# Scales of weights and tokens from sums of squares on ScalarE, and token operands turned in smaller DMAs, in a fused attention and mixture-of-experts kernel

## The chip, the cores and the metric

The kernel runs on one core of one Trainium2 chip. The metric is the time of one execution on the device in microseconds (us), as the median of several runs. PE is the matrix engine (TensorE), PEld its loads of weights, DVE is VectorE, ACT is ScalarE, POOL is GpSimd, and SP is the engine whose queue issues most DMAs. L1244 is line 1244 of the kernel before. The clock that PE was granted is given as a share of full speed, 2.4 GHz; its lower level is 1.2 GHz.

## What is computed

A windowed attention over 8 batches, 8 heads, 576 positions and 64 channels gives `x` of 4608 tokens by 512. Each token then goes to the two best of 8 experts, by noisy logits; an expert is a two-layer network of 512 to 1024 to 512, and a token's two results are added with its two weights. Cut to what matters here:

```python
scores = np.where(mask, scale * q @ k.T + bias, -1e9)      # window of 128 positions
attn = np.exp(scores - scores.max(-1)); attn /= attn.sum(-1) + 1e-9
x = (attn @ v)                                              # 4608 x 512
top2 = np.argpartition(-noisy_logits, 2, axis=1)[:, :2]
for e in range(8):
    for k in range(2):
        mask = top2[:, k] == e
        h = np.maximum(x[mask] @ w1[e], 0.0)
        out[mask] += top2_w[mask, k, None] * (h @ w2[e])
```

## The kernel before, in words

The products of the experts run in float16. An operand is scaled by a power of two and split into a high and a low half, so that hi*hi + hi*lo + lo*hi comes near to a product in float32. A scale must be known before anything can be split. For an expert's two weight matrices it is one number per matrix: `size_of_weights` (L1223) loads them once more in eight pieces of 128x1024 (`mraw`, a ring of two tiles), `largest` (L1230) takes the largest absolute value of each row of a piece on DVE (L1244), `powers_of_weights` (L1249) takes the maximum over all partitions with the help of PE (`of_all`, L484) and `floor_powers` (L495) keeps the exponent. For tokens it is one number per row: `turn_pair` (L1305) takes it for two gathered tiles of 128 tokens at a time, by a maximum on DVE (L1333).

Every expert but the first has three blocks of tokens: two wide ones of 512 and a narrow rest. A wide block's first product is done with seven smaller products in place of eight, by sums and differences of quarters of its operands. So `turn_pair` forms three more quarters (L1327 to L1331) on DVE or POOL, whichever the plan chooses, scales and splits 4 + 3 quarters into `hi` and `lo` tiles of 128x1792 (tiles `th`, `thw`, `tlw`; a ring of two pairs), and `across` (L1398) has SP issue one transposing DMA for each of the two tiles, 14 chunks of 128 columns at once, into the operand `blk.x` (tiles `xhw`, `xlw` or `xhe`, `xle`). Two pairs make a wide block, so that a block's operands come by four such DMAs.

In the products, `up_wide` (L1443, matmuls at L1434) writes banks that DVE and ACT add up and empty (`first_sum` to `halves_of`, lines 1479 to 1528: tiles `c`, `hh` and `hl`; line 277 is ACT's copy and line 279 DVE's), and `downs` (matmuls at L1564) multiplies `hh` and `hl` by the second weights. The narrow block's matmuls are at L1408 and L1569. Weights of an expert are loaded in chunks (`raw`, L1270 on SP's queue), scaled and split (L279 or L277 for the high half, L1276 for the low half, L1126 and L1141 for sums of them) into twelve sets of tiles, of which an expert takes eight.

The order on each engine isn't left to a scheduler. At build time the class `Order` plays the program through with estimated durations: a step is a strand of a coroutine that asks for an engine with a rank, the ready request with the lowest rank is issued first, and what comes out is the fixed order of every engine and of SP's queue. Ranks are numbers at the head of the file (`STAGE`, `GATE`, `SIZES`, `LATE`, ...), and durations stand beside each request. `either` (L261) and `added` let the plan choose between ACT and DVE, or DVE and POOL. On the chip every engine runs its rows strictly in that order and waits where a semaphore isn't there yet.

## Time and profile before

| | us |
|---|---|
| median of 3 runs | 1077.29 (1075.73 to 1081.77) |
| the profiled execution, its own time | 1077.1 |
| span of that execution, first to last instruction | 1075.4 |
| PE busy | 975.8 (91%) |
| DVE busy | 897.6 (83%) |
| ACT busy | 495.8 (46%) |
| POOL busy | 552.2 (51%) |
| mean granted clock of PE | 0.977 of full speed |

The profiled execution lies within 0.2 us of the median. Attention and routing take about the first 210 us, the first expert (in three blocks of its own, narrower kind) goes to about 330 us, and the seven others, about 100 us each, go on to the end. Busy shares are means over parts with different limits, so the stretches in which PE stands idle are read one by one below.

### The profile page before, as it was taken

What the parts mean: (1) busy time and instruction counts of PE and PEld (TensorE: products, weight loads), DVE (VectorE), ACT (ScalarE), POOL (GpSimd) and SP (SyncE); (2) the same over time, 40 slices, a digit from 0 to 9 for tenths busy, and PEclk for the clock granted to TensorE, in tenths of its full rate; (3) what the DMA queues carried; (4) which work ended last, traced back from release to release, by engine and by line L of the source; (5) the groups of instructions that cost most, each with busy time, mean ns of one, the idle gap of its engine ahead of it and who ended that gap; (6) DMA issues with size and microseconds to landing.
All of it is one profiled execution on the core that took longest, in us unless ns stands there. A gap on an engine that the chain in (4) does not pass through costs nothing. (4 is left out here: it accounts for less than half of the span.)

```text
span 1075.4 us, 24441 instructions
## 1 busy us (share of the span) xinstructions
PE 975.8 (91%) x8656; PEld 670.7 (62%) x8656; DVE 897.6 (83%) x2655; ACT 495.8 (46%) x1364; POOL 552.2 (51%) x767
## 2 busy tenths in 40 slices
PE   8999999799787899989988999899789989989996
PEld 5776666565356666766666656666656676657663
DVE  8999999997558999889799979998688979898530
ACT  8997987742123534353334333433433353434221
POOL 3458786654242456465464445555456456464022
PEclk9999999999898999999989999999999999998998
DMA  8869889642898499685969497857986897967023
GB/s 321 277 213 302 296 251 346 172 134 41 223 181 164 111 220 201 112 222 156 167 131 215 136 180 174 202 156 141 114 234 165 157 196 205 140 137 130 11 40 48
DMA packets 234540, 188.82 MB, mean 176 GB/s; under 512 B 145264, under 2 KB 188560, under 8 KB 234416
## 3 DMA queue, kind: packets, MB, share of 16 engines
q1 hardware_dynamic: 217072, 148.30, 53.7%
q0 software_dynamic: 17344, 38.94, 19.6%
q8 instruction: 68, 1.11, 0.4%
q14 instruction: 56, 0.46, 0.1%
HBM read 116.24 MB, written 40.71 MB: 146 GB/s over the span
## 5 line engine op out<-in xcount | busy, mean ns | idle before, releaser
L1668 POOL DMA_INDIRECT out_dram<-yo,ix x69 | 120.2, 1742 | 125.9 <-ACT yo L277 75.9
L1564 PEld LDWEIGHTS <-hh 128*128 128x128 f16 x896 | 86.9, 98 | 84.0 <-ACT hh L1533 1.4
L1533 ACT ACTIVATE hh<-bank 128x256 f16<-128x256 f32 (+8 forms) x136 | 47.8, 354 | 182.0 <-PE bank L1408 115.4
L1434 PEld LDWEIGHTS <-wth 128*128 128x128 f16 x896 | 87.8, 99 | 36.1 <-issue 16.9
L1564 PE MATMUL bank<-w2ha,hh 128*128 128x512 f16 x288 | 109.2, 379 | 0.9 <-ACT hh L1533 0.9
L1564 PE MATMUL bank<-w2ha,hl 128*128 128x512 f16 x288 | 109.2, 379 | 0.8 <-DVE hl L1523 0.8
L1564 PE MATMUL bank<-w2la,hh 128*128 128x512 f16 x288 | 109.2, 379 | 0.0
L556 ACT ACTIVATE p<-p,nm 128x128 f32<-128x128 f32 x256 | 99.3, 397 | 2.2 <-DVE nm L532 2.2
L1533 ACT ACTIVATE hh<-c 128x512 f16<-128x512 f32 (+1 forms) x96 | 48.5, 534 | 101.5 <-DVE c L1505 85.9
L1500 POOL TENSOR_TENSOR c<-c 128x256 f32<-128x256 f32 x33 | 38.4, 1164 | 101.2 <-DVE c L1497 78.7
L277 ACT ACTIVATE c<-bank 128x256 f32<-128x256 f32 x104 | 38.7, 379 | 94.0 <-PE bank L1434 93.7
L1564 PEld LDWEIGHTS <-hl 128*128 128x128 f16 x448 | 43.8, 98 | 54.0 <-DVE hl L1523 1.3
L1434 PE MATMUL bank<-xhw,wth 128*128 128x256 f16 x224 | 62.2, 278 | 14.4 <-DVE hl L1513 9.1
L1244 DVE TENSOR_REDUCE wam<-mraw 128x1 f32<-128x1024 f32 x56 | 67.0, 1207 | 2.2 <-DMA mraw<-in_w_dram 2.2
L1285 POOL DMA_INDIRECT xp<-xs_dram,ix x35 | 39.0, 1115 | 57.0 <-DVE ix L1034 38.6
L589 POOL TENSOR_SCALAR_AFFINE_SELECT pT<-pT 128x256 f32<-128x256 f32 (+1 forms) x80 | 42.8, 535 | 48.9 <-ACT pT L277 46.7
L532 DVE CUSTOM_DVE_ANT_0 p<-bank,bias 128x128 f32<-128x128 f32 x288 | 66.9, 283 | 0.4 <-ACT p L556 0.3
L1434 PE MATMUL bank<-xhw,wtl 128*128 128x256 f16 x224 | 62.1, 277 | 1.5 <-DVE wtl L1141 1.5
L1434 PE MATMUL bank<-xlw,wth 128*128 128x256 f16 x224 | 62.1, 277 | 0.0
L1408 PEld LDWEIGHTS <-w1ha 128*128 128x128 f16 x544 | 48.4, 99 | 21.0 <-issue 8.1
L1434 PE MATMUL bank<-xhe,wth 128*128 128x256 f16 x224 | 61.1, 273 | 0.1
L1434 PE MATMUL bank<-xhe,wtl 128*128 128x256 f16 x224 | 61.1, 273 | 0.0
(337 smaller groups left out, 3302.2 us busy)
## 6 DMA issues: line engine op xcount, KB each, us to landing
raw<-in_w_dram SPq DMA_DIRECT2D x144, 256.0 KB, 4.3
mraw<-in_w_dram SPq DMA_DIRECT2D x56, 512.0 KB, 5.0
qk<-in_qk_dram SPq DMA_DIRECT2D x32, 576.0 KB, 6.2
vraw<-in_v_dram SPq DMA_DIRECT2D x16, 640.0 KB, 5.7
out_dram<-xg SPq DMA_DIRECT2D x10, 1024.0 KB, 8.4
xs_dram<-x SPq DMA_DIRECT2D x32, 256.0 KB, 4.4
out_dram<-yo,ix POOLq DMA_INDIRECT x69, 6.6
xs_dram<-x SPq DMA_DIRECT2D x8, 128.0 KB, 6.3
```

Source lines behind the costliest of these rows:

```text
L277: nc.scalar.activation(o, i, AF.Copy, **kw)
L532: nc.vector.tensor_tensor_reduce(out=o, in0=i, in1=by, scale=-0.125, scalar=3.0e38, op0=OP.add, op1=OP.min, accum_out=m)
L556: nc.scalar.activation(pv, pv, AF.Exp, bias=nm[:, z, h:h + 1], scale=-1.0, accum_out=den[:, i, 2 * g + h:2 * g + h + 1])
L589: nc.gpsimd.affine_select(b, a, pattern, OP.is_ge, nothing, base=0, channel_multiplier=-1)
L1244: yield dve(us, rank, lambda: nc.vector.tensor_reduce(o, v, axis=AX.X, op=OP.max, apply_absolute_value=True))
L1285: nc.gpsimd.indirect_dma_start(out=o, out_offset=None, in_=xs[0:blk.rows], in_offset=bass.IndirectOffsetOnAxis(ap=blk.at[0:r, j:j + 1], ax ...
L1408: nc.tensor.matmul(t[:, 0:blk.n], wp[:, c], x[:, c, 0:blk.n], start=c == 0 and z == 0, stop=c == 3 and z == 2)
L1434: nc.tensor.matmul(t, wp[:, at + kc], xp[:, 2 * o + kc], start=not add and kc + z == 0, stop=kc + z == 3, skip_group_check=add)
L1500: yield added(ADD, ADDP, rank - MIDDLE, LATE[14], lambda e: e.tensor_tensor(c[:, 4], c[:, 0], c[:, 1], op=OP.add))
L1533: nc.scalar.activation(o, i, AF.Relu)
L1564: nc.tensor.matmul(blk.y[j], h[:, cs], wp, start=a == 0 and z + m == 0, stop=a == 3 and z + m == 3)
L1668: ins = nc.gpsimd.indirect_dma_start(out=out, out_offset=bass.IndirectOffsetOnAxis(ap=blk.ix[0:r, j:j + 1], axis=0), in_=t[0:r], in_offset ...
```

## The change

The largest absolute value gives way to a sum of squares. For each `mraw` piece of the last seven experts and for each pair of token tiles, ACT squares the 128x1024 values with an accumulated sum (`AF.Square`, `accum_out`), in place of DVE's maximum. The new `floor_roots` halves the exponent of that sum, which gives a power of two near its root; it has three short DVE instructions where `floor_powers` had two. The square of a token pair writes its unused output into the `hi` tile, so that the pair takes its `hi` and `lo` tiles from their ring ahead of the square and not after the powers. Each of the two parts (4 and 3 quarters) is then scaled, split and turned by itself: two DMAs of 8 chunks and two of 6 per pair, in place of two of 14. The numbers that set ranks, and some estimated durations, are new throughout; the first expert and the narrow blocks keep their maxima.

```diff
-LOAD = -335.2
+LOAD = -38.0
...
-STAGE = (-15.4, -3.6, 17.9, -92.5, -1.2, 202.6, 11.5, 11.9)
+STAGE = (15.5, 15.8, 6.0, -74.2, -13.5, 652.7, 124.4, 17.2)
...
-SIZES = (58.9, -13.8, 1095.7)
-SOON = -206.8
+SIZES = (33.6, -229.1, 1265.2)
+SOON = -104.9
...
-TURN, MARGIN, LATE_BY = (1.4, 0.3), 1.0, 1.0
-PACE, READ_BY, AHEAD = 0.9, 2.0, 13.8
+TURN, MARGIN, LATE_BY = (0.3, 0.3), 1.0, 1.0
+TURNED = 7e4
+PACE, READ_BY, AHEAD = 0, 2.0, -2.3
...
+    def floor_roots(ex_, squares):
+
+        nc.vector.tensor_scalar(ex_, squares, 0x7F800000, 1, op0=OP.bitwise_and, op1=OP.arith_shift_right)
+        nc.vector.tensor_scalar(ex_, ex_, float(127 << 22), None, op0=OP.add)
+        nc.vector.tensor_scalar(ex_, ex_, 0x7F800000, None, op0=OP.bitwise_and)
...
-                    spawn(largest(rg, t, t, 1.13, rank, wam[:, e % 2, z, q:q + 1],
-                                  (z, q, e), done))
+                    spawn(largest(rg, t, t, 1.11, rank, wam[:, e % 2, z, q:q + 1],
+                                  (z, q, e), done, AF.Square))
...
         if sum_:
-            yield act(us, rank, lambda: nc.scalar.activation(v, v, AF.Abs, accum_out=o))
+            yield act(us, rank, lambda: nc.scalar.activation(v, v, sum_, accum_out=o))
...
-                    yield pool(1.04, rank, lambda: gather(q + 2 * i, 128, xp[:, i * XW:i * XW + XW]))
+                    yield pool(1.25, rank, lambda: gather(q + 2 * i, 128, xp[:, i * XW:i * XW + XW]))
...
-        yield dve(1.2, rank, lambda: V.tensor_reduce(big, rows, axis=AX.XY, op=OP.max, apply_absolute_value=True))
+        hi, lo = yield (tpr, rank)
+        nothing_ = hi[:, 0:4 * HALF].rearrange("p (a b) -> p a b", a=2)
+        yield act(1.12, rank, lambda: nc.scalar.activation(nothing_, rows, AF.Square, accum_out=big))
...
-        for at_, src, n_ in parts_:
-            yield dve(0.13 + n_ * 0.267, rank, lambda at_=at_, src=src, n_=n_: V.scalar_tensor_tensor(
+            yield dve(0.13 + n_ * 0.267, rank, lambda: V.scalar_tensor_tensor(
                 shaped(lo, at_, n_), src, up_, shaped(hi, at_, n_), op0=OP.mult, op1=OP.subtract))
-        put(fitr, m)
-        put(xpr, xp)
-        mark(blk.weighed)
-        yield order.now + MARGIN
-        landed = Event(2)
-        for src, to in ((hi, blk.x[0]), (lo, blk.x[1])):
-            spawn(across(src, to[:, :, q * 128:q * 128 + 128], rank, landed, 4.5e5))
+            if z:
+                put(fitr, m)
+                put(xpr, xp)
+                mark(blk.weighed)
+            for t, to in ((hi, blk.x[0]), (lo, blk.x[1])):
+                spawn(across(t[:, at_], to[:, 8 * z:8 * z + 2 * n_, cs], rank, landed))
...
-        end = yield Op((("SP", TURN[0], rank),), lambda: nc.sync.dma_start_transpose(to, src))
-        yield order.transfer(end, size)
+        chunks_ = src.shape[1] // 128
+        end = yield Op((("SP", 0.2 + TURN[0] * chunks_, rank),), lambda: nc.sync.dma_start_transpose(to, src))
+        yield order.transfer(end, size * chunks_)
...
-        yield pool(1.08, rank, scatter)
+        yield pool(1.9, rank, scatter)
```

What the new numbers do to the order is seen in the rows of the queues. The rows of SP's queue below are those at the change from the fourth to the fifth wide expert (about 757 to 783 us in the profile of before), where `raw` are loads of weights, `mraw` loads for the weights' sizes, and `xhe` and `xle` the operands of the expert's second wide block; rows that only set an address register are left out. Before:

```order
L1270 DMA raw_121<-in_w_dram 128x512
L1400 DMA_TRANSPOSE xhe<-thw 128x14x128
L1270 DMA raw_119<-in_w_dram 128x4x128
L1270 DMA raw_122<-in_w_dram 128x512
L1400 DMA_TRANSPOSE xle<-tlw 128x14x128
L1270 DMA raw_120<-in_w_dram 128x4x128
L1400 DMA_TRANSPOSE xhe<-th 128x14x128
L1400 DMA_TRANSPOSE xle<-th 128x14x128
L1270 DMA raw_123<-in_w_dram 128x512
L1270 DMA raw_118<-in_w_dram 128x4x128
L1270 DMA raw_121<-in_w_dram 128x512
```

The same place in the changed kernel, from its sixth `raw` load after the first block's operands on:

```order
L1277 DMA raw_123<-in_w_dram 128x512
L1277 DMA raw_118<-in_w_dram 128x4x128
L1277 DMA raw_121<-in_w_dram 128x512
L1246 DMA mraw_4352<-in_w_dram 128x1024
L1246 DMA mraw_4353<-in_w_dram 128x1024
L1830 DMA list_4347<-slots_dram 128x1
L1277 DMA raw_4344<-in_w_dram 128x4x128
L1277 DMA raw_122<-in_w_dram 128x512
L1246 DMA mraw_4352<-in_w_dram 128x1024
L1246 DMA mraw_4353<-in_w_dram 128x1024
L1409 DMA_TRANSPOSE xhe<-thw 128x8x128
L1409 DMA_TRANSPOSE xle<-tlw 128x8x128
```

The four transposes stood among the loads of weights; now ten `raw` loads and four `mraw` loads stand ahead of the first of eight.

The rows of DVE below stand in the first wide block of the fourth wide expert (about 684 to 691 us in the profile of before): `wam` holds the rows' maxima, `w1hb`, `w1lb` and `w2lb` are scaled weights. Before:

```order
L1244 TENSOR_REDUCE wam<-mraw_4329 128x1
L1244 TENSOR_REDUCE wam<-mraw_4330 128x1
L1513 SCALAR_TENSOR_TENSOR hl_261<-bank_67,hh_258 128x256
L1505 TENSOR_TENSOR c_4319<-bank_68,c_4319 128x256
L1505 TENSOR_TENSOR c_4319<-bank_66,c_4319 128x256
L279 TENSOR_SCALAR w1hb_4292<-raw_4321,wsc 128x512
L1535 TENSOR_SCALAR hh_258<-c_4319 128x256
L1523 SCALAR_TENSOR_TENSOR hl_4284<-c_4319,hh_4281 128x512
```

And in the changed kernel:

```order
L1522 SCALAR_TENSOR_TENSOR hl_261<-bank_68,hh_258 128x256
L1514 TENSOR_TENSOR c_4342<-bank_66,c_4342 128x256
L1514 TENSOR_TENSOR c_4342<-bank_67,c_4342 128x256
L1354 SCALAR_TENSOR_TENSOR th<-xg,fit_255,th 128x1024
L1532 SCALAR_TENSOR_TENSOR hl_4307<-c_4342,hh_4304 128x512
L280 TENSOR_SCALAR w1hb_4315<-raw_4344,wsc 128x512
L1522 SCALAR_TENSOR_TENSOR hl_261<-c_4342,hh_258 128x256
```

The two maxima are gone from ahead of the low halves and sums; a token split (`th`) stands among them instead, which the order before had at an earlier place.

The rows of ACT at that same expert's first steps, where `hh` are the high halves after the first product and `c` are copies out of a bank. Before:

```order
L277 ACTIVATE yo_250<-bank_73,gw_244 32x512
L1533 ACTIVATE hh_259<-bank_67 128x256
L277 ACTIVATE wth_4316<-ts,wsc 128x1024
L1533 ACTIVATE hh_257<-c_4318 128x512
L1533 ACTIVATE hh_259<-c_4318 128x256
L277 ACTIVATE c_4319<-bank_67 128x256
L277 ACTIVATE c_4319<-bank_68 128x256
```

And in the changed kernel:

```order
L278 ACTIVATE yo_4345<-bank_73,gw_244 32x512
L1542 ACTIVATE hh_259<-bank_68 128x256
L1249 ACTIVATE mraw_4352,wam<-mraw_4352 128x1024
L1542 ACTIVATE hh_257<-c_4341 128x512
L1542 ACTIVATE hh_259<-c_4341 128x256
L1249 ACTIVATE mraw_4353,wam<-mraw_4353 128x1024
L278 ACTIVATE c_4342<-bank_68 128x256
L278 ACTIVATE c_4342<-bank_66 128x256
```

Squares of `mraw` stand ahead of `hh` and of the copies `c` out of the banks. Over the whole program DVE's rows have 84 of the maxima fewer, and ACT's 84 squares more; the plan gives DVE 26 more rows for `hh`, 25 more plain copies, 13 more scaled ones, 18 more token sums and 7 more sums of `c`, and 35 further short rows for the roots. ACT has 64 copies and `hh` rows fewer. POOL has 25 tensor rows fewer. SP has 154 transposes, not 98. PE's rows are as many as before.

## Rows read from the trace of the kernel before

**Rows 1.** The page's busy times: us, share of the span, instructions.

```profile
PE 975.8 (91%) x8656; PEld 670.7 (62%) x8656; DVE 897.6 (83%) x2655; ACT 495.8 (46%) x1364; POOL 552.2 (51%) x767
```

**Rows 2.** Two long stretches: us, PE, PEld, DVE, ACT, POOL busy; PE clock, DMA share, GB/s.

```profile
0.00:210.00 210.00, 192.17 (x2681) 134.59 (x2683) 197.50 (x1088) 180.58 (x736) 133.77 (x295) 0.99 0.84 277
...
362.00:1003.00 641.00, 589.47 (x4535) 412.85 (x4535) 568.51 (x1193) 252.92 (x482) 340.31 (x365) 0.98 0.78 165
```

**Rows 3.** Stretches again, the short ones in which PE stands idle most.

```profile
310.00:332.00 22.00, 12.07 (x73) 7.31 (x71) 9.99 (x25) 3.51 (x6) 3.77 (x3) 0.78 0.89 148
...
362.00:400.00 38.00, 35.17 (x239) 23.15 (x239) 36.21 (x83) 15.41 (x29) 20.32 (x18) 1.00 0.74 158
...
466.00:500.00 34.00, 29.40 (x214) 20.51 (x213) 33.23 (x70) 13.11 (x27) 21.22 (x23) 1.00 0.67 184
...
552.00:576.00 24.00, 17.95 (x176) 16.85 (x176) 23.38 (x55) 10.70 (x20) 12.25 (x16) 0.86 1.02 165
576.00:600.00 24.00, 20.14 (x147) 14.15 (x146) 23.55 (x51) 10.02 (x21) 12.78 (x15) 1.00 0.62 177
...
672.00:704.00 32.00, 27.79 (x210) 20.63 (x211) 31.62 (x72) 13.34 (x26) 17.07 (x19) 1.00 0.76 178
...
760.00:800.00 40.00, 29.69 (x285) 23.73 (x283) 26.07 (x48) 15.43 (x32) 17.40 (x19) 0.96 1.06 205
...
864.00:902.00 38.00, 32.56 (x315) 25.28 (x313) 32.15 (x71) 17.64 (x36) 18.96 (x20) 1.00 0.91 204
...
960.00:982.00 22.00, 15.30 (x178) 14.02 (x176) 17.49 (x39) 8.89 (x20) 10.62 (x14) 0.82 1.03 160
```

**Rows 4.** The maxima of L1244 alone in four of these stretches: length, DVE busy.

```profile
362.00:400.00 38.00, 2.40 (x2) 1.00 0.74 158
...
466.00:500.00 34.00, 3.61 (x3) 1.00 0.67 184
...
672.00:704.00 32.00, 3.59 (x4) 1.00 0.76 178
...
864.00:902.00 38.00, 2.42 (x2) 1.00 0.91 204
```

**Rows 5.** Groups by form: operands xcount, busy us, mean ns, idle before.

```profile
L1668 POOL DMA_INDIRECT out_dram<-yo,ix x69 | 120.2, 1742 | 125.9 <-ACT yo L277 75.9 <-issue 19.5 <-DVE yo L279 14.2
...
L1244 DVE TENSOR_REDUCE wam<-mraw 128x1 f32<-128x1024 f32 x56 | 67.0, 1207 | 2.2 <-DMA mraw<-in_w_dram 2.2
...
L277 ACT ACTIVATE thw<-xp,fit 128x1024 f16<-128x1024 f32 x13 | 14.9, 1144 | 11.4 <-DVE fit L1320 6.8 <-issue 4.6
```

**Rows 6.** Line 1242, ACT's sums in the first expert: duration ns min/median/max.

```profile
L1242 ACT ACTIVATION_READ_ACCUMULATOR raw<-raw x8: 196/222/247, 37.5 to 62.4; 128x1 f32 x8
```

**Rows 7.** Waits, DVE and PE: us in total, times, longest.

```profile
DVE c L1486 <- ACT c L277: 26.2, 10, 5.2
DVE fit L1333 <- DMA xg<-xs_dram,ix: 11.5, 2, 10.6
...
PE bank L1434 <- DVE c L1486: 16.5, 19, 2.6
```

**Rows 8.** SP's queue in time from 762 us on: start us, us.

```profile
762.56 5.01 SPq L1400 DMA_TRANSPOSE xle<-tlw  x1
...
768.68 8.86 SPq L1400 DMA_TRANSPOSE xhe<-th  x1
777.64 2.94 SPq L1400 DMA_TRANSPOSE xle<-th  x1
```

**Rows 9.** The chain of waits in the same place: start us, us.

```profile
767.77 10.38 DMA raw<-in_w_dram
...
782.04 5.79 DMA raw<-in_w_dram
```

**Rows 10.** Line 1400, SP's issue of a transpose: ns min/median/max (4 chunks, then 14).

```profile
L1400 SPq DMA_TRANSPOSE xh<-th x6: 1165/1192/1895, 301.8 to 902.0; - x6
...
L1400 SPq DMA_TRANSPOSE xhe<-thw x7: 1420/2844/4302, 366.5 to 963.6; - x7
```

More of the change, by code (lines that the diff above doesn't have):

```diff
@@ L42 @@
 BLOCKS = tuple(((FROWS, c - FROWS),) if z < NF else ((0, WIDE), (WIDE, WIDE), (2 * WIDE, c - 2 * WIDE)) for z, c in enumerate(CAPS))
-ZERO, EMPTY = -130.9, -14
-LOAD = -335.2
-VALUES = 122.0
-GATE = (-3.1, 151.9, 166.7, -14.0)
-ROUTE = (18.8, 43.4, 244.2, 76.5)
-SCATTER = (145.0, -808.8, -1083.1, -984.4, -235.6)
-FFN0, FFN1 = 162.9, 230.6
-WEIGHTS = (291.6, 237.2)
-TOKENS = 158.0
-STAGE = (-15.4, -3.6, 17.9, -92.5, -1.2, 202.6, 11.5, 11.9)
-MIDDLE = 85.9
-RESULT = -101.2
-SIZES = (58.9, -13.8, 1095.7)
-SOON = -206.8
+ZERO, EMPTY = -329.7, -14
+LOAD = -38.0
+VALUES = 209.5
+GATE = (0.4, 73.1, 284.5, 7.8)
+ROUTE = (2.4, 2.6, 29.4, 203.0)
+SCATTER = (255.9, -630.6, -1257.2, -856.7, -418.4)
+FFN0, FFN1 = 186.5, 215.7
+WEIGHTS = (236.3, 319.7)
+TOKENS = 294.0
+STAGE = (15.5, 15.8, 6.0, -74.2, -13.5, 652.7, 124.4, 17.2)
+MIDDLE = 156.3
+RESULT = -192.9
+SIZES = (33.6, -229.1, 1265.2)
+SOON = -104.9
 TIGHT = (1, 5, 7)
 QUICK = (5, 7)
-LATE = (-176.8, 77.1, 84.6, 140.9, -80.7, -281.1, -2.3, -181.3, 169.4, -15.8, 36.4, 137.7, -84.5, -99.0, -30.4)
+LATE = (-111.2, -284.7, 64.4, 270.8, -378.0, -448.0, -39.9, -178.4, 120.6, -73.6, 73.3, -28.7, -196.6, -140.2, 78.6)
 LAG = 0.2
-ADD, ADDP, TWS = 0.36, 0.8, 5
-BEHIND = 4.2
-TURN, MARGIN, LATE_BY = (1.4, 0.3), 1.0, 1.0
-PACE, READ_BY, AHEAD = 0.9, 2.0, 13.8
+ADD, ADDP, TWS = 0.36, 0.9, 5
+BEHIND = 5.0
+TURN, MARGIN, LATE_BY = (0.3, 0.3), 1.0, 1.0
+TURNED = 7e4
+PACE, READ_BY, AHEAD = 0, 2.0, -2.3
 HELD = 3
-SWITCH, NEAR = 0.093, 2.5
+SWITCH, NEAR = 0.093, 4.4
 TOP, SOFT, SPLIT = (1.27, 1.52, 0.92), (1.56, 1.56, 0.8), (0.85, 1.35, 0.85)
@@ L1209, in early_sizes @@
                     spawn(largest(rg, t, v, (0.6, 0.7)[z], SIZES[e], wam[:, e % 2, z, f:f + 1],
-                                  dram(src, e * DM * F + f * 65536, [[512, 128], [1, 512]]), done, z))
+                                  dram(src, e * DM * F + f * 65536, [[512, 128], [1, 512]]), done, AF.Abs if z else None))
             yield done
@@ L1224, in size_of_weights, with largest @@
                     yield order.now + PACE
-                    spawn(largest(rg, t, t, 1.13, rank, wam[:, e % 2, z, q:q + 1],
-                                  (z, q, e), done))
+                    spawn(largest(rg, t, t, 1.11, rank, wam[:, e % 2, z, q:q + 1],
+                                  (z, q, e), done, AF.Square))
             yield done
             yield from powers_of_weights(e, rank)
-    def largest(rg, t, v, us, rank, o, src, done, sum_=False):
+    def largest(rg, t, v, us, rank, o, src, done, sum_=None):
         def from_():
@@ L1253, in powers_of_weights @@
         a, wide = yield from of_all(wmx, 2, rank)
-        yield dve(0.14, rank, lambda: floor_powers(wex[:, e], wide))
+        yield dve(0.3, rank, lambda: (floor_powers if e < EARLY else floor_roots)(wex[:, e], wide))
         put(tb, a)
@@ L1301, in tokens @@
             xg = yield (xgr if early else xpr, rank)
-            yield pool(1.04, rank, lambda: gather(j, r, xg[0:r, 0:XW]))
+            yield pool(1.25, rank, lambda: gather(j, r, xg[0:r, 0:XW]))
             spawn(turn_tokens(blk, j, r, xg, rank))
@@ L1317, in powers @@
         def powers():
-            floor_powers(big.bitcast(I32), big.bitcast(I32))
+            floor_roots(big.bitcast(I32), big.bitcast(I32))
             V.tensor_scalar(up_.bitcast(I32), big.bitcast(I32), -1.0, float(256 << 23), op0=OP.mult, op1=OP.add)
@@ L1340, in turn_pair @@
         shaped = lambda t, at_, n_: t[:, at_].rearrange("p (a b) -> p a b", a=2) if n_ == 4 else t[:, at_]
-        for at_, src, n_ in parts_:
+        landed = Event(4)
+        cs = slice(q * 128, q * 128 + 128)
+        for z, (at_, src, n_) in enumerate(parts_):
             yield either(0.2 + n_ * 0.21, 0.13 + n_ * 0.133, rank, LATE[6],
-                         lambda e, at_=at_, src=src, n_=n_: copy(e, shaped(hi, at_, n_), src, scale=up_))
-        for at_, src, n_ in parts_:
-            yield dve(0.13 + n_ * 0.267, rank, lambda at_=at_, src=src, n_=n_: V.scalar_tensor_tensor(
+                         lambda e: copy(e, shaped(hi, at_, n_), src, scale=up_))
+            yield dve(0.13 + n_ * 0.267, rank, lambda: V.scalar_tensor_tensor(
                 shaped(lo, at_, n_), src, up_, shaped(hi, at_, n_), op0=OP.mult, op1=OP.subtract))
-        put(fitr, m)
-        put(xpr, xp)
-        mark(blk.weighed)
-        yield order.now + MARGIN
-        landed = Event(2)
-        for src, to in ((hi, blk.x[0]), (lo, blk.x[1])):
-            spawn(across(src, to[:, :, q * 128:q * 128 + 128], rank, landed, 4.5e5))
+            if z:
[4 more added lines that the diff above has]
+                spawn(across(t[:, at_], to[:, 8 * z:8 * z + 2 * n_, cs], rank, landed))
         yield landed
@@ L1396, in turn_tokens, with across @@
         mark(blk.ready)
-    def across(src, to, rank, landed, size=1.3e5):
-        end = yield Op((("SP", TURN[0], rank),), lambda: nc.sync.dma_start_transpose(to, src))
-        yield order.transfer(end, size)
+    def across(src, to, rank, landed, size=TURNED):
+        chunks_ = src.shape[1] // 128
+        end = yield Op((("SP", 0.2 + TURN[0] * chunks_, rank),), lambda: nc.sync.dma_start_transpose(to, src))
+        yield order.transfer(end, size * chunks_)
         yield order.now + TURN[1]
```

3 lines of the change are left out of this document (1 added, 2 removed).

## The prediction

> **What bounds the kernel now.** I read the page's busy times first, then the long stretches, then the short ones, then waits and chain. The page [rows 1] shows PE busy for 975.8 of 1075.4 us and DVE for 897.6: PE is the bound, DVE comes close behind it, and ACT has half its time free. The long stretches [rows 2] tell where. In attention, up to 210 us, PE, DVE and ACT are all busy for 180 to 198 us; no maximum that goes stands there, so I expect nothing of it. From 362 to 1003 us, most of the seven wide experts, PE is busy for 589.47 of 641 us, DVE for 568.51 and ACT for only 252.92. The prize is in those 51.5 us of idle PE and a few more before. An expert takes some 100 us; for most of it PE never stops, and what is won on DVE there is worth nothing. The short stretches [rows 3] hold the idle time, and they are of two kinds.
>
> DVE-bound ones: from 362, 466, 552, 576, 672 and 864 us (38, 34, 24, 24, 32 and 38 us, 190 in all) DVE is busy for 36.2, 33.2, 23.4, 23.6, 31.6 and 32.2 us, while PE idles for 2.8, 4.6, 6.1, 3.9, 4.2 and 5.4, together 27.0. There an expert begins: its weights are scaled and split on DVE while its first product already waits for sums on DVE.
>
> Stretches bound by transfers: from 310, 760 and 960 us PE idles for 9.9, 10.3 and 6.7 us, with DVE far from full and DMA at 0.89 to 1.06 of 16 engines. From 760 us the queue of SP explains it: transposes hold SP for 5.01, 8.86 and 2.94 us [rows 8], loads of weights stand behind them, and the chain waits 10.38 and 5.79 us for two of these [rows 9]. From 310 us DVE stands for 10.6 us at a token maximum whose gather is late [rows 7].
>
> **DVE's relief.** 84 maxima go, 56 of weights and 28 of token pairs, at 1207 ns [rows 5]: 101 us. The plan spends much of it again: 89 further rows come to DVE, and 35 short ones. At the mean of its instructions from 362 to 1003 us (568.51 / 1193, 0.48 us [rows 2]) the 89 cost 42 us; the short ones cost from almost nothing to the same mean, 17 us. So DVE gets 42 to 59 us lighter; I take 54. Spread over the 680 us or so of the wide experts that is 8%, or 15 us of the 190 in DVE-bound stretches. Counted otherwise, the maxima of weights that really stood in four of them sum to 2.40 + 3.61 + 3.59 + 2.42 = 12.0 us [rows 4]. Either number lies below the 27 us that PE idles there, so each can be PE's in full. I take 15; the ends are 5, if what the plan put back stands in the same places, and 27.
>
> **The order of SP.** At the fourth to fifth wide expert ten loads of weights now go ahead of the second block's operands, where two went before. The 10.38 and 5.79 us of waiting leave the chain, of which PE's idle time was 10.3 us. I take 8; ends 0 (another transfer is late in their place) and 10.3. The pair from 310 us keeps its wait: the gather is as late as it was, only the square on ACT stands at it and DVE's token sums behind the square, hence 0. From 960 us two token maxima of 1.2 us each [rows 5] go from the chain to a narrow product: 2 of 6.7 us.
>
> **The clock.** The granted clock was 0.86, 0.96 and 0.82 in the stretches from 552, 760 and 960 us [rows 3], that is, partly at 1.2 GHz after PE had stood still. Against full speed it lost 24 x 0.14 + 40 x 0.04 + 22 x 0.18 = 9 us. With half the idle time gone, I take back 4; ends 0 and 9.
>
> **What is added.** ACT: 84 squares of 128x1024. No row shows one; the nearest is ACT's scaled copy of that size, 1144 ns, plus 196 to 222 ns for reading the sum [rows 5, 6], or 1.34 us: 113 us. The 64 rows that leave ACT bring 34 back (0.52 us each, 252.92 / 482 [rows 2]). ACT rises by 79 us to some 575, and its free time covers them: from 362 to 1003 us it is busy for 39%. Without that cover they cost what the second rival says; in the sum they cost 0. Behind each waits a row of `hh` or `c` on ACT; the pair's square also waits for a free `th` or `thw` tile now, earlier than before.
>
> SP: 56 transposes more. SP's issue of 4 chunks takes at least 1165 ns and of 14 at least 1420 [rows 10], so 26 ns for a chunk; 8 and 6 chunks would take 1.27 and 1.22 us, and each split costs 1.07 us more, 60 us in all. Most of it lies where nothing waits for SP. I charge a twentieth, 3 us; ends 0 and the third rival's. In return the first part is turned while the second is split, which nothing waits for in a block that is one block ahead: 0.
>
> **Ranks.** They move everything a little, in attention too. The rows give no price; I bound it by 10 us either way. In favour, the plan now counts 1.9 us for a scatter, which takes 1742 ns [rows 5] and was counted as 1.08.
>
> **The sum.** 15 + 8 + 2 + 4 - 3 = 26 us less than the profiled execution's 1077.1 us, which lies 0.2 us below the median: **1051 us**. Its own range is 1028 to 1067.
>
> **The rivals.** *Freed time falls where PE is full.* Of DVE's 54 us only those in stretches with idle PE count, and the two waits at weights there may simply move to the next low half. For it: of the 67.0 us that the maxima of weights take [rows 5], only the 12.0 us above lie in four of the stretches with idle PE. Against it: DVE is 95 to 99% busy in five of the six stretches. It gives the lower ends, 5 + 0 and no clock, so 1077 - 5 + 3 = 1075, and up to 1067.
>
> *ACT takes DVE's place* (slower). ACT issues in order, and squares stand ahead of `hh` and `c`. PE waited 16.5 us for sums of `c` on DVE, and those 26.2 us for `c` copies on ACT [rows 7], so that this path is near the edge already. Each expert has 12 squares of 1.34 us; where an expert begins, a quarter of them delays a copy that PE needs: 7 x 3 x 1.34 = 28 us. The waits for gathers, 11.5 us on DVE, move to ACT. With DVE's 15 and the SP term of 8 won, that gives 1077 + 28 + 11 - 23 = 1093. It decides once a square starts less than 1.3 us ahead of the copy behind it. Against it: ACT has 60% free and the plan knows of the squares, at 1.11 us.
>
> *The added transposes are paid.* Four more stand ahead of each expert's loads of weights: 7 x 4 x 1.07 = 30 us, with the SP term lost and DVE's relief kept, 1077 - 19 + 30 = 1088. For it: DMA is over 1.0 busy in three of the stretches [rows 3], and the 14-chunk row has a median twice its minimum [rows 10]. Against it: a queue that is full is filled by bytes, which stay the same. The Trainium skill speaks for this rival, in "DMA: Bandwidth & Descriptors", "Rules for kernel authors": many small transfers should be made one large one; no row here shows a part turned in two pieces. By that rule the split is a loss without a return, the time 1088; by the rows it is 3 us.
>
> That the change doesn't do what it says is out: the queues show the squares and the split parts.
>
> **How the numbers follow.** Forecast 0.60 (0.58 of it faster, 0.02 the same), freed time lost 0.18 (0.10 faster, 0.08 the same), ACT in DVE's place 0.13, transposes paid 0.09 (0.02 of it faster when ACT and DVE make up for it). A difference of 0.5%, 5.4 us, is about what a measurement can tell from no change. Faster: 0.58 + 0.10 + 0.02 = 0.70; the same: 0.10; slower: 0.13 + 0.07 = 0.20. The range runs from 1028 (the forecast's lower end) to 1086, which takes in the first rival and leaves out most of the two slower ones.
>
> **What would show it.** Right: DVE's busy time near 845 us, ACT's near 575, PE's idle time down from 100 to some 75, no wait of PE longer than 3 us near the fifth expert's start. Squares near 1.3 us with their sum. Wrong: PE idle as before with DVE below 90% in the stretches where experts begin (freed time lost), waits of DVE sums for `c` on ACT above 26 us with squares ahead of them (ACT), or SP's transposes summing to over 60 us more with loads landing late behind them.

## The result, and the profile after

The changed kernel takes 1066.55 us (median of 4, 1066.22 to 1068.48) against 1079.53 (4 runs, 1075.73 to 1083.01): a ratio of 0.9884, 95% interval 0.9843 to 0.9925. It is 1.2% faster where 2.4% was forecast. The profiled execution has a span of 1066.8 us, 8.6 us under the one of before, while the medians differ by 13.0: the rows below account for the 8.6. Its busy times, beside [rows 1]:

```profile
PE 977.8 (92%) x8656; PEld 666.6 (62%) x8656; DVE 850.0 (80%) x2695; ACT 557.0 (52%) x1468; POOL 525.6 (49%) x742
```

DVE fell by 47.6 us (845 us was forecast) and ACT rose by 61 (575). So the work moved nearly as worked out, and yet PE's idle time within the span went from 99.6 to 89.0 us, not to 75. The stretches tell where. The start of an expert is taken here as the first product of the wide first layer (line 1434 before, 1443 now) after the last product of the expert ahead. The first wide expert starts at 354.7 us before and at 344.7 now; PE's last product ends at 1065.8 and 1056.3. Columns as in [rows 2]; the stretch ahead of that start and the one behind it, first before, then after:

```profile
210.00:354.70 144.70, 125.02 (x949) 78.75 (x944) 105.96 (x319) 43.66 (x109) 60.54 (x87) 0.93 0.65 147
354.70:1065.80 711.10, 658.59 (x5036) 457.33 (x5034) 594.11 (x1251) 270.90 (x521) 356.43 (x385) 0.98 0.74 153
```

```profile
210.00:344.70 134.70, 124.17 (x984) 79.22 (x977) 97.10 (x333) 47.95 (x108) 65.22 (x96) 0.99 0.70 151
344.70:1056.30 711.60, 659.00 (x5037) 453.06 (x5034) 554.33 (x1286) 327.77 (x620) 331.27 (x362) 0.99 0.69 155
```

This is the result of the two profiles in four rows. Ahead of the first wide expert 10.0 us are won. In the seven wide experts, where I had put all of my 26 us, DVE gives up 40 us, and PE's busy time and the length stay: 711.1 and 711.6.

Inside the wide experts idle time only moved. The sums over all seven, before and then after, of the 15 us ahead of a start, of the first 35 us, and of the 50 us behind those:

```profile
sum 105.00, PE 88.78 PEld 80.51 DVE 91.59 ACT 41.44 POOL 61.26; mean PE 12.68 PEld 11.50 DVE 13.08 ACT 5.92 POOL 8.75
sum 245.00, PE 210.76 PEld 151.23 DVE 218.01 ACT 106.93 POOL 115.86; mean PE 30.11 PEld 21.60 DVE 31.14 ACT 15.28 POOL 16.55
sum 350.00, PE 345.80 PEld 221.30 DVE 278.73 ACT 115.61 POOL 172.20; mean PE 49.40 PEld 31.61 DVE 39.82 ACT 16.52 POOL 24.60
```

```profile
sum 105.00, PE 97.30 PEld 83.86 DVE 62.01 ACT 45.61 POOL 76.34; mean PE 13.90 PEld 11.98 DVE 8.86 ACT 6.52 POOL 10.91
sum 245.00, PE 209.96 PEld 141.20 DVE 225.37 ACT 124.74 POOL 120.62; mean PE 29.99 PEld 20.17 DVE 32.20 ACT 17.82 POOL 17.23
sum 350.00, PE 338.63 PEld 224.59 DVE 269.37 ACT 155.91 POOL 129.15; mean PE 48.38 PEld 32.09 DVE 38.48 ACT 22.27 POOL 18.45
```

PE's idle time went from 16.2 to 7.7 us ahead of a start, from 34.2 to 35.0 behind it, and from 4.2 to 11.4 in the middle. DVE was freed by 30 us ahead of the starts and became busier behind them. The splits of the token pairs (their low halves, line 1345, now 1354) did most of that; their DVE time in the 15 us ahead and in the first 35, before and after:

```profile
sum 105.00, DVE 29.68; mean DVE 4.24
sum 245.00, DVE 7.03; mean DVE 1.00
```

```profile
sum 105.00, DVE 5.31; mean DVE 0.76
sum 245.00, DVE 33.88; mean DVE 4.84
```

The maxima of the weights, 14.76 us of those 245, left; 27 us of token splits came. What each row costs now, beside [rows 5]:

```profile
L1249 ACT ACTIVATE mraw<-mraw 128x1024 f32<-128x1024 f32 x56 | 58.5, 1045 | 1.6 <-DMA mraw<-in_w_dram 1.6
L1249 ACT ACTIVATION_READ_ACCUMULATOR mraw<-mraw 128x1 f32 x56 | 10.6, 189 | 0.0
```

1.23 us for a square with its sum, where I took 1.34.

**The place of the 10 us.** Before, DVE stood 10.63 us at a token maximum [rows 7], whose two gathers took 13.6 us to land (median), and PE stood 9.93 at its product for the low halves `hl` of the first expert, which stand behind that maximum in DVE's order. In time, from POOL's, SP's and DVE's queues, before (its last line is PE's wait: us in total, times, longest) and then after:

```profile
308.99 1.01 POOL L1285 DMA_INDIRECT xg<-xs_dram,ix  x1 [0.30 <-DVE wam L1244]
310.30 1.86 POOL L1285 DMA_INDIRECT xg<-xs_dram,ix  x1 [0.30 <-issue]
310.52 4.96 SPq L1400 DMA_TRANSPOSE xhw<-thw  x1
315.52 9.99 SPq L1400 DMA_TRANSPOSE xlw<-tlw  x1
324.03 1.22 DVE L1333 TENSOR_REDUCE fit<-xg 128x1 f32<-128x1024 f32 x1 [10.63 <-DMA xg<-xs_dram,ix]
...
326.76 1.21 DVE L1244 TENSOR_REDUCE wam<-mraw 128x1 f32<-128x1024 f32 x1
327.89 0.74 DVE L1548 SCALAR_TENSOR_TENSOR hl<-bank,hh 128x256 f16<-128x256 f32 x2
...
PE bank L1557 <- DVE hl L1548: 9.9, 1, 9.9
```

```profile
310.15 1.01 POOL L1292 DMA_INDIRECT xg<-xs_dram,ix  x1 [0.30 <-issue]
311.47 0.97 POOL L1292 DMA_INDIRECT xg<-xs_dram,ix  x1 [0.30 <-issue]
316.33 2.25 SPq L1409 DMA_TRANSPOSE xhw<-thw  x1
320.89 1.06 ACT L1342 ACTIVATE th<-xg 128x1024 f16<-128x1024 f32 x1 [1.76 <-DMA xg<-xs_dram,ix]
```

Before, the first turn (transposing DMA) of the first pair began while the second gather was still being issued, 0.2 us behind it, and the second turn 5.0 us later; now the turns begin 4.9 us behind that gather's issue, and what waits for the gathers, a square on ACT, waits 1.76 us.

### The profile page after: what moved, and what is told of

It is laid out like the page before. It is cut to its first block, busy times and chain, and to the rows that moved or that the text cites. A ratio compares the mean times of both kernels' runs of the same rounds, so it can differ in the third digit from the quotient of the medians.

```text
span 1066.8 us, 24641 instructions
## 1 busy us (share of the span) xinstructions
PE 977.8 (92%) x8656; PEld 666.6 (62%) x8656; DVE 850.0 (80%) x2695; ACT 557.0 (52%) x1468; POOL 525.6 (49%) x742
## 3 DMA queue, kind: packets, MB, share of 16 engines
q0 software_dynamic: 17344, 38.94, 18.8%
## 5 line engine op out<-in xcount | busy, mean ns | idle before, releaser
L1677 POOL DMA_INDIRECT out_dram<-yo,ix x69 | 112.9, 1637 | 115.3 <-ACT yo L278 79.3
L1542 ACT ACTIVATE hh<-bank 128x256 f16<-128x256 f32 (+8 forms) x124 | 44.2, 358 | 171.1 <-PE bank L1417 105.9
L1542 ACT ACTIVATE hh<-c 128x512 f16<-128x512 f32 (+1 forms) x82 | 42.9, 536 | 73.4 <-DVE c L1514 55.2
L1557 DVE SCALAR_TENSOR_TENSOR hl<-bank,hh 128x384 f16<-128x384 f32 (+8 forms) x88 | 31.5, 363 | 58.6 <-ACT hh L1542 45.3
L1509 POOL TENSOR_TENSOR c<-c 128x256 f32<-128x256 f32 x26 | 26.3, 1011 | 86.9 <-DVE c L1506 57.3
L278 ACT ACTIVATE c<-bank 128x256 f32<-128x256 f32 x84 | 31.1, 378 | 69.3 <-PE bank L1443 67.4
L278 ACT ACTIVATE yo<-bank,gw 128x512 f32<-128x512 f32 (+4 forms) x63 | 42.8, 684 | 42.3 <-PE bank L1573 22.6
L518 PE MATMUL bank<-qk 64*64 64x192 f32 (+1 forms) x1024 | 56.9, 334 | 7.9 <-DVE raw L359 4.7
L1573 PE MATMUL bank<-w2hb,hl 128*128 128x512 f16 x160 | 60.7, 379 | 1.7 <-DVE hl L1532 1.7
```

What stands on the lines that cost most here:

```text
L278: nc.scalar.activation(o, i, AF.Copy, **kw)
L518: nc.tensor.matmul(s[h][a:a + 64, o + first_:o + first_ + c_], qk[half, i * 128 + a:i * 128 + a + 64], qk[half, QW + k0 + first_:QW + k0 + ...
L1509: yield added(ADD, ADDP, rank - MIDDLE, LATE[14], lambda e: e.tensor_tensor(c[:, 4], c[:, 0], c[:, 1], op=OP.add))
L1542: nc.scalar.activation(o, i, AF.Relu)
L1557: yield dve(0.07 + c * 0.00104, rank - MIDDLE, lambda: nc.vector.scalar_tensor_tensor(hl[:, 0:c], t[:, 0:c], 0.0, hh[:, 0:c], op0=OP.max, ...
L1573: nc.tensor.matmul(blk.y[j], h[:, cs], wp, start=a == 0 and z + m == 0, stop=a == 3 and z + m == 3)
```

## The experiments

"Order held" means that every engine's queue has the same rows in the same order, but for the rows named. Times are ratios to the kernel before on the same chip. "Start" is the first wide expert's start, "wide" the time from there to PE's last product, "idle" PE's idle time in the first 35 us of the seven wide experts, all from the one trace of each run. The diffs are cut to the lines that matter.

| run | ratio, 95% interval | DVE | ACT | start | wide | idle |
|---|---|---|---|---|---|---|
| before | 1 | 897.6 | 495.8 | 354.7 | 711.1 | 34.2 |
| changed | 0.9884 [0.9843, 0.9925] | 850.0 | 557.0 | 344.7 | 711.6 | 35.0 |
| squares of weights in place | 0.9899 [0.9868, 0.9931] | 841.3 | 552.2 | 348.8 | 707.8 | 31.8 |
| all squares in place | 0.9887 [0.9856, 0.9918] | 816.3 | 580.1 | 344.1 | 711.6 | 32.5 |
| squares beside the maxima | 0.9972 [0.9946, 0.9998] | 895.8 | 582.5 | 347.7 | 714.6 | 35.6 |
| first turns later | 0.9956 [0.9931, 0.9980] | 897.6 | 495.2 | 347.0 | 712.4 | 37.6 |
| no low tokens | 0.9939 [0.9912, 0.9966] | 850.7 | 495.1 | 354.0 | 703.1 | 31.2 |
| no low weights | 0.9790 [0.9749, 0.9830] | 836.1 | 495.5 | 360.2 | 692.3 | 26.5 |
| two turns (in before) | 0.9993 [0.9963, 1.0023] | 897.4 | 496.6 | 354.9 | 715.0 | 34.3 |
| numbers only | 0.9974 [0.9948, 0.9999] | 891.6 | 501.0 | 367.9 | 691.5 | 26.5 |
| numbers, squares in place | 0.9967 [0.9942, 0.9993] | 836.5 | 557.2 | 370.7 | 687.1 | 21.2 |
| changed, maxima in place | 1.0340 [1.0304, 1.0376] | 929.1 | 471.1 | 346.7 | 754.5 | 43.2 |
| changed, copy before squares | 1.0049 [1.0018, 1.0081] | 846.5 | 639.4 | 347.8 | 731.6 | 34.1 |
| changed, one turn, planned | 0.9983 [0.9959, 1.0006] | 853.1 | 551.0 | 349.9 | 721.8 | 35.8 |
| changed, again | 0.9895 [0.9846, 0.9945] | 847.1 | 556.5 | 343.0 | 711.1 | 35.8 |
| changed, one turn | 0.9835 [0.9788, 0.9882] | 846.2 | 556.6 | 342.6 | 703.4 | 32.1 |
| changed, one turn, again | 0.9882 [0.9841, 0.9923] | 847.5 | 556.5 | 343.6 | 708.5 | 33.8 |

The last rows repeat two kernels. The two traces of one turn differ by 5 us in "wide", so differences of that size between single traces say little by themselves.

**Squares of weights in place.** The kernel before, order held; the weights' maxima become squares at their places.

```diff
-            yield dve(us, rank, lambda: nc.vector.tensor_reduce(o, v, axis=AX.X, op=OP.max, apply_absolute_value=True))
+            yield dve(us, rank, lambda: nc.scalar.activation(v, v, AF.Square, accum_out=o) if us > 1 else
+                      nc.vector.tensor_reduce(o, v, axis=AX.X, op=OP.max, apply_absolute_value=True))
```

> The kernel before with its order held row for row; only the 56 maxima of the weights become squares on ACT, at the same places. DVE loses 56 x 1.2 = 67 us and ACT gains 56 x 1.3 = 75 us. Theory A (the relief of DVE is worth something where experts begin, and the changed kernel's new order spends it again): 8 to 15 us faster than before, 1063 to 1070, with PE's idle time in the first 35 us of the seven wide experts down from 34 us to about 22. Rival B (the freed time falls where PE is full in any order): within 4 us of before. Rival C (squares on ACT delay the copies of c and hh): slower than before by 5 us or more.

1.0% faster, as theory A had it; but 5.9 us of it lie ahead of the first wide expert, and PE's idle time where experts begin fell by 2.4 us, not by 12, though 14.76 us of maxima left these very stretches. The long wait near 320 us was gone.

**All squares in place.** The same for the token pairs too, written to a tile that nothing reads.

```diff
-        yield dve(1.2, rank, lambda: V.tensor_reduce(big, rows, axis=AX.XY, op=OP.max, apply_absolute_value=True))
+        yield dve(1.2, rank, lambda: nc.scalar.activation(waste[0], rows, AF.Square, accum_out=big))
```

> The kernel before with its order held; all 84 maxima become squares on ACT at their places (those of the token pairs write to a tile that nothing reads). The 56 of the weights alone gave 9 us. Theory A (DVE's time counts where experts begin): half as much again for half as many squares more, 3 to 6 us below that run, 1063 to 1066. Rival (the gain was the one long wait for a gather at 310 us, which those 56 moved): no more than 1 us below it. Rival C (squares on ACT delay copies): above it.

No more than the weights alone, within the intervals, as the rival had it. This run has the whole swap without a new plan or split turns, and it equals the changed kernel in the ratio, in the start and in the length of the wide experts. The 81 us off DVE, with the squares on ACT, brought nothing in the length of the wide experts. Much of the freed time became waiting on DVE: its sums `c` waited 26.2 us for ACT's copies before [rows 7], and wait 46.4 in this run.

```profile
DVE c L1493 <- ACT c L277: 46.4, 18, 5.2
```

**Squares beside the maxima.** Nothing leaves DVE; ACT gets the squares too.

```diff
-        yield dve(1.2, rank, lambda: V.tensor_reduce(big, rows, axis=AX.XY, op=OP.max, apply_absolute_value=True))
+        yield dve(1.2, rank, lambda: (V.tensor_reduce(big, rows, axis=AX.XY, op=OP.max, apply_absolute_value=True),
+                                      nc.scalar.activation(waste[0], rows, AF.Square, accum_out=waste[1])))
```

> The kernel before with its order held and all 84 maxima kept; beside each, a square on ACT whose result nothing uses. It prices ACT's part alone: ACT gains 84 x 1.2 = 104 us, DVE loses nothing. The run with squares in the maxima's places was 1.1% faster than before. If ACT's part is free, as the prediction had it: within 3 us of before. By the run with a copy ahead of every square (92 us of ACT for some 18 us): 15 to 20 us slower; then DVE's relief alone is worth some 25 to 30 us and ACT takes back more than half.

Near the first case, 3 us faster by the ratio, and far from the second: more work made the kernel no slower. The start came 7.0 us earlier, at 347.7, and the wide experts took 3.5 us more. On SP the first pair's turns stand behind two loads of `mraw`, and these now wait until a square on ACT has read the tile as well: the second load was issued at 310.76 instead of 310.14, the first turn at 311.15 instead of 310.52. The gathers were issued at 308.38 and 309.70, 0.6 us earlier than before, landed in 7.0 us, and DVE's wait fell to 3.52 us. The sums `c` waited 28.4 us for ACT's copies, so the 46.4 above come with a DVE that has less to do, not with squares alone. Against this run the one with all squares in place prices DVE's relief alone, in that order: 0.9887 against 0.9972, 0.85% or 9 us; the two profiles have 6.6 us between the ends of PE's last products, 3.6 of it ahead of the first wide expert.

**First turns later.** Only SP's order changes, at one place: the first pair's two turns go behind the second pair's first.

```diff
+        def turn():
+            if keep_:
+                kept.append((to, src))
+                return
+            nc.sync.dma_start_transpose(to, src)
+            while kept:
+                nc.sync.dma_start_transpose(*kept.pop(0))
```

> The kernel before with all maxima on DVE; one thing moved: the two turns of the first wide block's first pair go behind the first turn of its second pair on SP, so that they don't run while the second pair's gathers are under way. Theory E (the gain of the change is that one wait: the gathers lay 13.6 us beside these turns, DVE stood 10.6 us at the maximum behind them and PE 9.9): 6 to 10 us faster than before, though nothing leaves DVE. Theory A (DVE's relief): no change, or slower by up to 5 us because the block's operands come later.

0.44% faster with every maximum on DVE, 4.7 us where theory E had 6 to 10; the start lies at 347.0. From the queues of this run:

```profile
309.18 1.01 POOL L1285 DMA_INDIRECT xg<-xs_dram,ix  x1 [0.30 <-DVE wam L1244]
310.50 1.86 POOL L1285 DMA_INDIRECT xg<-xs_dram,ix  x1 [0.30 <-issue]
317.74 1.22 DVE L1333 TENSOR_REDUCE fit<-xg 128x1 f32<-128x1024 f32 x1 [4.14 <-DMA xg<-xs_dram,ix]
324.86 1.51 SPq L1406 DMA_TRANSPOSE xhw<-th  x1
```

The gathers, issued as before, landed in 7.2 us instead of 13.6, and PE's gap was 3.45 us instead of 9.93. Some 7.7 of the 10.0 us that the change wins ahead of the first wide expert are to be had by moving two transposes. The other runs in the order of before agree. Where the first turn still begins 0.2 us behind the second gather (before, two turns, no low tokens, no low weights), DVE waits 10.0 to 13.6 us for it and the start is at 354.0 or later. Where it begins 1.45 to 2.2 us behind it (squares beside the maxima, and in place), the wait is 2.1 to 5.4 us and the start at 348.8 or earlier.

**No low tokens, no low weights.** Two runs that leave out DVE time at other places, 46.9 and 61.5 us of it: the low halves of the token pairs, and those of the weights, are computed in full once for each tile, and then for a few columns. Their output is of no use; they only price the time.

```diff
-                shaped(lo, at_, n_), src, up_, shaped(hi, at_, n_), op0=OP.mult, op1=OP.subtract))
+                few(shaped(lo, at_, n_)), few(src), up_, few(shaped(hi, at_, n_)), op0=OP.mult, op1=OP.subtract))
```

```diff
-        yield dve(0.66, rank, lambda: nc.vector.scalar_tensor_tensor(lo, t, sc, hi, op0=OP.mult, op1=OP.subtract))
+        yield dve(0.66, rank, lambda: nc.vector.scalar_tensor_tensor(few(lo), few(t), sc, few(hi), op0=OP.mult, op1=OP.subtract))
```

> The kernel before with its order held; the low halves of the token pairs are computed in full only once for each tile and for 16 of their columns after that (the output suffers). DVE loses some 55 us, nearly all of it in the 15 us before and the 35 us after an expert's start, where PE stands idle for 50 us in all. Theory A (DVE's load in that place is what PE waits for): 15 us or more faster than before. Rival D (PE waits there for a chain of short steps through ACT and DVE, or for transfers, however busy DVE is): at most 5 us.

> The kernel before with its order held; the low halves of the weights are computed in full only once for each tile, and after that for 4 of 512 columns (the output suffers). 105 rows of 0.74 us shrink, some 65 us of DVE, as much as the 56 maxima are (67 us). Theory F (DVE's load counts only where it stands in front of PE: while PE idled in the first 35 us of an expert, DVE spent 1.8 of 34.2 us on maxima and 7.2 on these low halves): 12 us or more faster than before, with the first 35 us of the seven experts losing 10 of their 34 us of idle PE. Rival D (PE waits there for steps that are late for other reasons, however much leaves DVE): at most 7 us, as where the low halves of the tokens were left out.

0.6% for 47 us of tokens, between its two cases, 2.1% for 61.5 us of weights; taking 80 us of maxima off was worth 0.85%. (Of the token rows only 29.68 + 7.03 us lay in the 50 us around the starts, not nearly all as the expectation had it.) The first 35 us of the experts, without the low tokens and without the low weights:

```profile
sum 245.00, PE 213.81 PEld 153.96 DVE 217.12 ACT 108.11 POOL 114.69; mean PE 30.54 PEld 21.99 DVE 31.02 ACT 15.44 POOL 16.38
```

```profile
sum 245.00, PE 218.51 PEld 157.11 DVE 193.15 ACT 109.13 POOL 113.28; mean PE 31.22 PEld 22.44 DVE 27.59 ACT 15.59 POOL 16.18
```

Without the low tokens DVE is as full there as before (218.01): other work moved up. Without the low weights 25 us leave the stretch, PE's idle time falls by 7.7 us there and by 11.2 in the 15 us ahead of the starts, and the wide experts take 18.8 us less, of which 5.5 go into a later start; the wait near 320 us is still there (12.87 us). So DVE's load is what PE waits for where experts begin, but more that of the expert's own weights than that of the maxima or tokens. The trace of before points to it: over the 34.2 us in which PE idles in these stretches, the rows of DVE that run meanwhile are 10.2 us of sums `c`, 8.9 of the weights' low halves at line 1276 (the expectation left out one of their four tiles), 3.8 of their summed ones, and 1.8 of maxima. In the 15 us ahead of the starts, though, these low halves run for only 0.75 us of PE's idle time, and 11.2 us were won there; how is not shown. And of who waits for line 1244, the maxima, and for line 1486, the sums:

```profile
who waited for it (us, times):
  POOL xg L1285: 0.6, 2
  PEld bank L511: 0.2, 1
```

```profile
  PE bank L1434: 16.5, 19
```

By the profile no product of an expert was released by a maximum. That leaves out rows that wait behind one in DVE's order, as `hl` did near 320 us behind two of them.

**Two turns, one turn.** The split by itself, put into the kernel before (8 and 6 chunks back to back), and taken out of the changed kernel with its order held (one turn where the second part's stands).

```diff
+                nc.sync.dma_start_transpose(to[:, 0:cut], src[:, 0:cut * 128])
+            nc.sync.dma_start_transpose(to[:, cut:], src[:, cut * 128:])
```

```diff
-                spawn(across(t[:, at_], to[:, 8 * z:8 * z + 2 * n_, cs], rank, landed))
+                spawn(across(t[:, at_], to[:, :, cs], rank, landed, whole=t if z else False))
```

> The changed kernel with its order held on every engine but SP: one transpose of 14 chunks where the second part's stands, instead of 8 and 6. If 56 added transposes cost what the prediction charged, 3 us: 1063 to 1065. If they cost nothing: 1066. If they are paid in full at four per expert, 30 us: 1040 or less. If turning the first part early is worth something: slower than the changed kernel by 2 us or more.

> The kernel before with its order held; only every turn of 14 chunks becomes one of 8 and one of 6, back to back. In the changed kernel the reverse edit gave 7 us. If the pieces cost that by themselves (SP's fixed time for each transpose): 5 to 10 us slower than before, 1083 to 1088. If the 7 us come from where the pieces stand in the new order: within 3 us of before.

> The changed kernel itself, on the same chip as the next run: 0.984 to 0.993 of before.

> The changed kernel with its order held and one turn of 14 chunks per half, beside the changed kernel on the same chip. If the split costs what the first look at it said: 5 to 8 us faster than the changed kernel. If that was the chip of that run, or chance: within 2 us of it, as the split by itself cost nothing in the kernel before.

The first run of one turn gave 0.9835 [0.9788, 0.9882], the second 0.9882 [0.9841, 0.9923] beside the changed kernel's 0.9895 [0.9846, 0.9945] on the same chip. The 7 us of the first run did not come again: 56 transposes more cost nothing that these runs can tell, in either order. One turn is, on its two runs, the fastest kernel that computes everything, by no more than the intervals.

**Numbers only, and numbers with squares in place.** The ranks and counted costs of the changed kernel in the code of before; then with its order held and the weights' squares in place.

```diff
-PACE, READ_BY, AHEAD = 0.9, 2.0, 13.8
+PACE, READ_BY, AHEAD = 0, 2.0, -2.3
...
-        yield pool(1.08, rank, scatter)
+        yield pool(1.9, rank, scatter)
```

> The kernel before with the ranks and planned costs of the changed kernel alone: maxima on DVE, single transposes. The time to the first wide expert's start was 354.7 us before and 344.7 after. Theory A: the 10 us up to there come from the ranks and the counted cost of gathers and scatters, so it starts there near 345 too; later it pays for the maxima, so 1068 to 1080 in all. Rival B (the ranks are the whole of the gain): 1064 to 1069. Rival C (the ranks need the squares): slower than before.

> The run with the changed kernel's numbers alone, its order held, and the 56 maxima of the weights as squares on ACT in their places. In the kernel before this edit gave 9 us, by way of one long wait near 310 us. If the relief of DVE is worth something in any order: 8 us or more below the numbers alone, 1066 or less. If it was that one wait: within 4 us of the numbers alone, 1071 to 1079, since this order has another long wait (16.5 us at 345 us, for the last maximum of the weights) that a square meets just as late.

The numbers alone are worth 0.3%: the wide experts take 19.6 us less, and the start comes 13.2 us later, behind a wait of PE of 16.5 us for the last maximum of the weights. The squares add nothing to it that the intervals tell apart; the wait is then 19.88 us. My claim that the start near 345 comes from the numbers fell here: the start of this run is at 367.9.

**Maxima in place of the squares, copy before the squares, one turn planned.** The changed kernel, order held, with DVE maxima where its squares stand; with an idle copy on ACT ahead of each square; and with one turn and the plan made anew.

```diff
-        yield act(1.12, rank, lambda: nc.scalar.activation(nothing_, rows, AF.Square, accum_out=big))
+        yield act(1.12, rank, lambda: V.tensor_reduce(big, rows, axis=AX.XY, op=OP.max, apply_absolute_value=True))
```

```diff
-            yield act(us, rank, lambda: nc.scalar.activation(v, v, sum_, accum_out=o))
+            yield act(us, rank, lambda: (us > 1 and nc.scalar.activation(v, v, AF.Copy),
+                                         nc.scalar.activation(v, v, sum_, accum_out=o)))
```

```diff
-            for t, to in ((hi, blk.x[0]), (lo, blk.x[1])):
-                spawn(across(t[:, at_], to[:, 8 * z:8 * z + 2 * n_, cs], rank, landed))
+            for t, to in ((hi, blk.x[0]), (lo, blk.x[1])) if z else ():
+                spawn(across(t, to[:, :, cs], rank, landed))
```

> The changed kernel with its order held; its 84 squares become maxima on DVE again, where the squares stood. DVE gains 84 x 1.2 = 101 us and goes to 950. Theory A: DVE is the bound where experts begin, so this costs 15 us or more over the changed kernel, 1082 or more. Rival B: at most 5 us over it, 1072, since DVE waits idle 15 us before an expert begins. Rival C: faster than the changed kernel, since ACT's copies come earlier.

> The changed kernel with its order held and an idle copy of 128x1024 on ACT ahead of each of the 84 squares: ACT gains 84 x 1.1 = 92 us. Rival C of the prediction (squares on ACT delay the copies that PE needs, a quarter of them at full price): 20 us or more slower, 1087 or more. Theory A (ACT has room; it is 52% busy): up to 6 us slower, 1066 to 1073.

> The changed kernel with one turn of 14 chunks per half, and the plan made anew for it, so that the order moves on every engine. Holding the order this gave 1059. If the split was the one loss in the change: 1055 to 1062. If how the ranks fall matters more than any single part: anything between 1045 and 1075.

The maxima cost 4.6% in this order, 43 us of it in the wide experts: the new order counts on a DVE without them, and PE waits longer for the sums `c`. So the swap of the same 84 rows is worth 1.1%, 12 us, in the order of before (all squares in place) and some 49 us in the new one; its price belongs to the order. From the waits of the changed kernel, and of this run:

```profile
PE bank L1443 <- DVE c L1495: 27.1, 20, 3.7
```

```profile
PE bank L1444 <- DVE c L1496: 45.8, 26, 4.0
```

Which rows had moved into the maxima's place was seen above. The copies cost 1.65%, 18 us for 82 us of ACT. In the profiles the wide experts take 20 us more, about half of it as idle time of PE, which in the middle of the experts went from 11.4 to 20.6 us. The other half is PE's busy time, 659.0 and now 669.6 us, at a granted clock of 0.99 and now 0.97. And a plan made anew, for a change that costs nothing by itself, lost 1%, outside both cases of its expectation.

## Why the prediction was wrong

- **"There an expert begins: its weights are scaled and split on DVE while its first product already waits for sums on DVE."** Right in the main, as the run without low weights shows. The step that failed is the next, 15 us for DVE's relief "spread over" these stretches, and the 12.0 us of maxima [rows 4] as a second count. Maxima stood in the stretches, but only 1.8 of PE's 34.2 idle us passed while one ran, and 14.76 us of them taken out of the first 35 us won 2.4. In the six stretches, moved along with the starts, PE's idle time fell from 27.0 to 22.8 us: 4 in place of 15. That came back too. Over the eight stretches in the wide experts PE's idle time fell from 44.0 to 31.4, and outside them, where I had written that for most of an expert "PE never stops", it rose from 8.5 to 21.2. Net, the wide experts won 0 (711.1 and 711.6), and DVE's relief alone is worth 9 us in the order of before. The prediction's own lower end, "if what the plan put back stands in the same places", is what the 27 us of token splits did.
- **"The pair from 310 us keeps its wait ... hence 0."** This is where nearly all of the profiled gain lay, 10.0 us. I took the late gather as given; it was late beside the first pair's turns, which the squares and the new order put later. That the time still fell, and fell inside the stated range, is luck: the gain came from a place that the sum had at nothing.
- **The order of SP, 8 us.** In the stretch from 760 us, moved along, PE's idle time fell from 10.3 to 6.2 us, and no wait in the fifth expert's first 35 us is longer than 2.67 where one was 4.73: 4 us. **From 960 us, 2 us:** there it fell from 6.7 to 2.4, but that expert's first 35 us went from 2.1 to 6.0. Both came, and the rest of the experts took them back.
- **The clock, 4 us.** The granted clock of the span rose from 0.977 to 0.982, but PE's busy time did not fall (975.8 and 977.8): 0. In attention alone it rose from 192.2 to 194.6, at 0.99 and 0.98. Since idle time only moved, little could come back; that the clock has a price is seen in the run with copies.
- **ACT at no cost.** Mis-sized. By the copies 82 us of ACT cost 18 us, where I had counted PE as safe: its idle time in the middle rose by 7.2 us in the changed kernel and by 3.9 with squares beside the maxima. The waits of DVE for ACT's `hh`, before and after, point the same way; that the squares made all of the 7.2 us is not shown. The second rival named the mechanism and put 28 us on it; it did not decide.

```profile
DVE hl L1548 <- ACT hh L1533: 31.0, 22, 5.4
DVE hl L1557 <- ACT hh L1542: 45.3, 30, 7.4
```

- **Transposes, 3 us.** 0 within the intervals, put in and taken out. The third rival falls. The Trainium skill's rule in "DMA: Bandwidth & Descriptors", section "Rules for kernel authors", by which many small transfers should be one large one, puts the overhead at transfers under 64 KB; the pieces here hold 256 and 192 KB, and splitting to these sizes cost nothing that the runs can tell. SP's rows are 1266 ns a piece now against the 2844 of the 14 chunks [rows 10].

```profile
L1409 SPq DMA_TRANSPOSE xhw<-thw x14: 1237/1266/2248, 316.3 to 927.9; - x14
```

- **Ranks, bounded by 10 us.** A plan made anew moved the time by 1% (one turn planned). The bound was right, and as wide as the result.
- **The rivals and the range.** The first rival, freed time that falls where PE is full, is nearest to what happened in the wide experts. It gave 1067 to 1075; the 10 us near 320 us, which no case had, bring the result just under it. The upper end of the forecast's own range, 1067, does not follow from the ends of its terms: 5 + 0 + 2 + 0 - 3 gives 1073.

## What to carry to other kernels

Before pricing work that leaves a busy engine, lay its rows over the idle time of the engine that sets the pace, and look at what stands behind them in the queue: here 1.8 of 34.2 us said beforehand that the maxima were hardly in the way where experts begin. This is a hint and no price: the swap of the same 84 rows was worth 12 us in one order and some 49 in another. Work that a plan already puts behind what is urgent gained little when it went, since the queue filled up with other rows or waited for another engine. And a single long wait is worth tracing to its transfer's neighbours first: two transposes, moved, gave 0.44%, with 84 reductions left where they were.

## What was unexpected of the hardware

- The same two gathers, issued at the same places, landed in 13.6 us (median) with two turns of 14 chunks beside them, the first issued 0.2 us behind the second gather and the other 5.0 us later, and in 7.2 us without them. With the first turn 1.45 us behind, as in the run with squares beside the maxima, they landed in 7.0 us. The two turns held SP for 4.96 and 9.99 us beside the gathers, and for 2.07 and 2.54 us when they were issued at 326 and 329 us.
- More work on one engine did not make the kernel slower: with 84 unused squares on ACT, 87 us, the first wide expert began 7 us earlier and the time was 0.28% shorter (interval 0.02 to 0.54%). In this run the loads of `mraw` ahead of the turns waited for the squares, and the turns moved off the gathers.
